# The last batch's second product by seven products of halves

## The chip, the cores and the metric

The kernel runs on one core of one Trainium2 chip. The metric is the device time of a whole run in microseconds; three runs of the kernel before gave 647.86, 649.02 and 649.75, so its time is the median, 649.02. The engines are PE (matrix products; PEld is its weight load), DVE (vector), ACT (scalar), POOL (GpSimd) and SP, whose queue issues every DMA of this kernel.

## The reference

Four batches of 768 positions and 512 channels go through an attention and then through a two-layer block. With float32 arrays throughout:

```
x  = attention(q, k, v)                 # banded, plus 24 block summaries; 8 heads of 64
h  = x.transpose(0,2,1) @ U @ V         # mixing over the positions, rank 32
u  = x + h.transpose(0,2,1)
ch = max(u @ w_ch1, 0) @ w_ch2          # 512 -> 2048 -> 512
return u + ch
```

The change is about `max(u @ w_ch1, 0) @ w_ch2`, the second product, for the last of the four batches. As a product of matrices it is 512 channels by 2048 hidden rows by 768 positions.

## The kernel before, in words

A float32 factor is used as two parts, a rounded high one and the rest (`hi`, `lo`), and each product is three matmuls: high by high, high by low, low by high. So every weight and every activation has to be split: ACT copies the high part into a rounding type, and another engine subtracts it for the low part.

Batch 0 runs both products directly while the weights are still arriving, and stores what the later batches need to DRAM: the first layer's weights with four sums of halves (`up_there`), and the second layer's weights (`down_there`). Batches 1 to 3 each run two phases.

- `up_phase` is the first product, already by seven products of halves instead of eight (Winograd's form of Strassen's scheme). The hidden rows go in eight pairs p; each pair takes seven products of six matmuls of 384 columns. A result is four blocks of 128x384 in `st.h[p]`. Two products of the last pair, `third` and `second`, are left over at its end and run among the first steps of the next phase.
- `down_phase` is the second product, direct. For each of 16 blocks f of 128 hidden rows, four output tiles of 512 columns and two of 2x256 (in the last batch four of 256) are accumulated in six to eight PSUM banks; the positions are 768 = 512 + 256. `gate_high` (line 1284, ACT) and `gate_low` (line 1288, DVE) make the two parts of max(h, 0) for the next f, in two buffers `gh` and `gl` of their own. `leave` (line 1339, DVE) adds u and sends the outputs.

The weights of both phases come back from DRAM as `whole` tiles of up to 512 KB by `fetch_weight` (line 884, three buffers) and are split into units of 128x512 by `prepare` (lines 179 and 180: the high part on ACT, the low part on POOL; eight buffers). `prepare` is called once for every unit that is used, so four units are ready ahead of use. `tick` fetches the next `whole` a few steps after the second unit of one is split.

The order on every engine is the order in which this code is written: nothing reorders it, and each engine works through its own queue, waiting on semaphores. While a batch runs its two phases, the attention of the next batch is spread between their steps (`later_steps`); the last batch has none beside it. The eight PSUM banks, and the buffers named `w…`, `op…` and `h…`, are used in turn by different tiles; a new user waits until the last reader of the old tile is done.

## Time and profile before

| | |
|---|---|
| three runs, median | 649.02 us (647.86 to 649.75) |
| the profiled execution | 648.17 us, of which the profile's span is 646.4 us |
| PE busy in the span | 627.1 us (97%), 5528 matmuls |
| DVE, ACT, POOL busy | 361.7, 354.6 and 363.3 us (55 to 56%) |
| the chain that ended last | PE 87%, DMA 4%, DVE 3% |
| granted TensorE clock | 1.00 in all stages |

The span is what lies between the first and the last instruction; 1.77 us of the run's own time lie around it. In a matmul row of the profile the duration is that from start to end of one matmul, and matmuls overlap, so what a matmul costs is read from a stretch with many of them: its length over their count. The stages of the span: batch 0 until about 216 us, batch 1 from there to 366, batch 2 to 517, batch 3 to the end; the last batch's first product is at 517 to 574 and its second at 574 to 643.

### The profile page before, as it was taken

How to read it: one execution, taken by the hardware profiler on the slowest of the kernel's cores; microseconds unless marked ns; L12 is line 12 of the kernel's file. 1: busy time of each engine (PE TensorE's matmuls, PEld its weight loads, DVE VectorE, ACT ScalarE, POOL GpSimd, SP SyncE). 2: the span in 40 equal slices, each digit the busy share in tenths (PEclk: the TensorE clock that was granted, in tenths of full speed). 3: DMA queues.
4: the chain of work that ended last, by engine and by line, in shares of the span. 5: the costliest groups of instructions: out<-in, count | busy, mean ns of one | idle time of the engine just before them, and what ended most of it. 6: DMA issues, size and time to landing. Idle time of an engine off the chain costs nothing.

```text
span 646.4 us, 14559 instructions
## 1 busy us (share of the span) xinstructions
PE 627.1 (97%) x5528; PEld 563.4 (87%) x5528; DVE 361.7 (56%) x1002; ACT 354.6 (55%) x788; POOL 363.3 (56%) x391
## 2 busy tenths in 40 slices
PE   5879999999999999999999999999999999999997
PEld 4669988888888899998888899998888899998886
DVE  5779767675857596566444645565544522242223
ACT  4756766656663657675453457775453455553321
POOL 3525977965766875862246765771344565653320
PEclk9999999999999999999999999999999999999999
DMA  9897588866675169896628367887431164342002
GB/s 236 223 380 222 160 296 267 229 201 189 214 232 176 46 213 290 243 265 174 180 78 218 113 204 222 258 258 203 144 116 58 60 183 142 115 131 66 32 1 99
DMA packets 68678, 115.39 MB, mean 179 GB/s; under 512 B 6912, under 2 KB 43648, under 8 KB 68608
## 3 DMA queue, kind: packets, MB, share of 16 engines
q1 hardware_dynamic: 68608, 114.45, 58.9%
q8 instruction: 44, 0.72, 0.5%
q14 instruction: 26, 0.21, 0.1%
HBM read 90.31 MB, written 24.12 MB: 177 GB/s over the span
## 4 chain that ended last, share of the span: by engine, by line
PE 87%; DMA 4%; DVE 3%; SPq 2%; ACT 2%; issue 1%; DVEq 0%; ACTq 0%
PE acc L1316 30%; PE ps_h L1215 27%; PE acc L949 10%; PE ps_h L927 9%; PE ps_x L490 3%; PE ps_s L374 2%; PE ps_s L351 2%; DMA place<-in_w 1%; PE ps_t L460 1%; SPq L215 1%; DMA kt<-in_k 1%; PE ps_u L699 1%; DMA place<-in_v 1%; DMA place<-in_q 1%; PE ps_m L665 1%
## 5 line engine op out<-in xcount | busy, mean ns | idle before, releaser
L180 POOL TENSOR_TENSOR parts<-whole,parts 128x512 fp32r<-128x512 f32 (+1 forms) x144 | 182.3, 1273 | 162.9 <-ACT parts L179 153.1
L1316 PE MATMUL acc<-gh,parts 128*128 128x256 f32 (+1 forms) x768 | 198.2, 340 | 0.0
L1215 PE MATMUL ps_h<-op,parts 128*128 128x384 f32 x1008 | 181.7, 337 | 0.1
L1215 PEld LDWEIGHTS ps_h<-op,parts 128*128 128x128 f32 x1008 | 174.3, 188 | 2.7 <-issue 1.1
L1316 PEld LDWEIGHTS acc<-gh,parts 128*128 128x128 f32 x768 | 132.9, 189 | 17.4 <-issue 1.7
L1316 PE MATMUL acc<-gl,parts 128*128 128x256 f32 (+1 forms) x384 | 129.8, 338 | 0.2
L1288 DVE SCALAR_TENSOR_TENSOR gl<-place,gh 128x768 fp32r<-128x768 f32 x48 | 55.3, 1151 | 71.3 <-ACT gh L1284 71.2
L179 ACT CAST parts<-whole 128x512 fp32r<-128x512 f32 (+1 forms) x144 | 83.3, 583 | 3.3 <-DMA whole<-up 1.0
L1316 PEld LDWEIGHTS acc<-gl,parts 128*128 128x128 f32 x384 | 72.8, 189 | 7.5 <-DVE gl L1288 0.8
L410 ACT ACTIVATE e<-e,neg 128x120 f32<-128x120 f32 x144 | 46.5, 386 | 51.4 <-DVE neg L400 46.9
L927 PE MATMUL ps_h<-place 128*128 128x384 f32 x384 | 74.3, 342 | 0.0
L1284 ACT ACTIVATE gh<-place 128x768 fp32r<-128x768 f32 x48 | 40.5, 844 | 57.1 <-PE acc L1316 48.5
L927 PEld LDWEIGHTS ps_h<-place 128*128 128x128 f32 x384 | 66.2, 188 | 1.4 <-issue 0.4
L949 PE MATMUL acc<-place,gh 128*128 128x512 f32 x192 | 67.3, 405 | 0.0
L155 POOL TENSOR_SCALAR val<-place 128x512 f32<-128x512 f32 (+1 forms) x30 | 47.7, 1607 | 25.9 <-ACT place L142 21.4
L180 POOL TENSOR_TENSOR place<-val,place 128x512 fp32r<-128x512 f32 x29 | 38.7, 1357 | 18.3 <-ACT place L179 18.3
L742 POOL TENSOR_TENSOR op<-tmp,op 128x384 fp32r<-128x384 f32 x24 | 26.3, 1108 | 32.9 <-ACT op L738 30.2
L949 PEld LDWEIGHTS acc<-place,gh 128*128 128x128 f32 x192 | 35.9, 188 | 7.6 <-POOL place L180 0.6
L400 DVE CUSTOM_DVE_ANT_0 e<-ps_s,mask_sb 128x120 f32<-128x120 f32 x144 | 32.8, 277 | 11.3 <-PE ps_s L351 5.9
L949 PE MATMUL acc<-place,gl 128*128 128x512 f32 x96 | 37.7, 393 | 0.1
L161 DVE SCALAR_TENSOR_TENSOR val<-place,val 128x512 int32<-128x512 int32 (+1 forms) x33 | 31.7, 965 | 3.3 <-POOL val L155 3.2
L1241 DVE TENSOR_TENSOR place<-place,ps_h 128x384 f32<-128x384 f32 x24 | 13.2, 551 | 36.2 <-PE ps_h L1215 36.2
(113 smaller groups left out, 796.5 us busy)
## 6 DMA issues: line engine op xcount, KB each, us to landing
place<-in_w SPq DMA_DIRECT2D x32, 512.0 KB, 5.6
whole<-up SPq DMA_DIRECT2D x24, 512.0 KB, 4.4
whole<-down SPq DMA_DIRECT2D x24, 512.0 KB, 4.3
whole<-up SPq DMA_DIRECT2D x24, 384.0 KB, 3.4
vt<-in_v SPq DMA_DIRECT2D x48, 146.2 KB, 3.8
kt<-in_k SPq DMA_DIRECT2D x24, 288.0 KB, 5.9
there<-squares SPq DMA_DIRECT2D x16, 384.0 KB, 4.3
at<-there SPq DMA_DIRECT2D x64, 96.0 KB, 3.5
```

What stands on the lines that cost most here:

```text
L155: nc.gpsimd.tensor_scalar(f32(bits), f32(hi), 0.0, None, ALU.mult)
L161: lambda lo, hi, bits: nc.vector.scalar_tensor_tensor(bits, lo, 29, bits, ALU.logical_shift_right, ALU.bitwise_or),
L179: nc.scalar.copy(hi, val)
L180: engine.tensor_tensor(lo, val, f32(hi), ALU.subtract)
L400: nc.vector.tensor_tensor_reduce(out=e[:, u, :], in0=ps[:, i * KC : (i + 1) * KC], in1=mask_sb[:, m, :], scale=-SCALE, scalar=BIG, op0=ALU ...
L410: nc.scalar.activation(e[:, u, :], e[:, u, :], AF.Exp, bias=st.neg[h][:, u : u + 1], scale=-1.0,)
L927: nc.tensor.matmul(ps[:, :NH], w_split[0, f][:, c % 2, part_w, c // 2], ut[:, c, :], start=(n == 0), stop=(n == 3 * NC - 1),)
L949: nc.tensor.matmul(acc[t], gt[:, sl], w_split[1, f][:, part_w], start=(first and j == 0), stop=(last and j == 2),)
L1215: nc.tensor.matmul(ps, a[:, sa, i], b[:, sb, i], start=(first and n == 0), stop=(n == 5), skip_group_check=not first,)
L1284: nc.scalar.activation(gh, h, AF.Relu)
L1288: nc.vector.scalar_tensor_tensor(gl, h, 0.0, f32(gh), ALU.max, ALU.subtract)
L1316: nc.tensor.matmul(place, w[:, part_w, c * P : (c + 1) * P], gt[:, q0:q1], start=(f == 0 and i == 0 and j == 0), stop=(f == NF - 1 and j = ...
```

## The change

The last batch's second product is done by the same seven-product form. The 16 hidden blocks are taken as eight pairs, the output channels and the positions as two halves each, so that a pair's weights are blocks B11, B12, B21, B22 of 128x256 and its activations four blocks of 128x384. The products run one after the other (`SEVEN`), each over all eight pairs: a step n = (product k, pair p) is six matmuls of 384 columns, and there are 56 steps. Sums are kept in six PSUM banks (x, y, z, two channel blocks each), and three of them carry on from one product to a later one.

- *Weights.* During batch 1's `down_phase`, `sum_down` makes T1 to T4 of every pair on POOL, four subtractions of 128x256, into `op` and `h` buffers that are free then, and SP stores them (line 960). During batch 2's `down_phase` the split parts of B11, B21 and B22 are stored as they are, three DMAs of 256 KB a pair. The last batch loads the B units ready split (one 512 KB DMA for a unit of two pairs, line 933) and the T sums whole; their high part is ACT's as before, their low part DVE's (line 949) and no longer POOL's, one step later.
- *Activations.* `gate_sums` (lines 1410 to 1415) takes the place of the gate for a pair: three max(h, 0) of 128x384 on ACT in place, and three sums on DVE. It runs in the last `up_phase`, one pair behind. In each step of the new phase the operand is split: high part on ACT (line 1433), low part on DVE (line 1440), up to twelve steps ahead, in 18 buffers. One more sum of each pair (`fourth_sum`, line 1444) is made in product 3.
- *Outputs.* Each half of a channel block is begun and ended by a DVE addition of 128x384 (lines 1465 and 1472) and sent as 192 KB.

PE's queue in the last phase, first as it was (a tile of 512 positions and one of 256; `acc` are the output tiles):

```order
L1316 MATMUL acc_7505<-gh,parts 128x512
L1316 MATMUL acc_7505<-gl,parts 128x512
L1316 MATMUL acc_7505<-gh,parts 128x512
L1316 MATMUL acc_7516<-gh,parts 128x256
L1316 MATMUL acc_7516<-gl,parts 128x256
L1316 MATMUL acc_7516<-gh,parts 128x256
```

These stand among 384 such matmuls, 192 of each width. As they are now, from the end of the last `up_phase` (L1291) on:

```order
L1291 MATMUL ps_h<-op,parts 128x384 x324
L1501 MATMUL acc<-gh,parts 128x384 x6
L1291 MATMUL ps_h<-op,parts 128x384 x6
L1501 MATMUL acc<-gl,parts 128x384 x6
L1291 MATMUL ps_h<-op,parts 128x384 x6
L1501 MATMUL acc<-gh,parts 128x384 x6
L1501 MATMUL acc<-gl,parts 128x384 x6
L1501 MATMUL acc<-gh,parts 128x384 x6
L1501 MATMUL acc<-place,parts 128x384 x60
```

The 192 matmuls of 512 columns and 192 of 256 have become 336 of 384, with the two left-over products between the first steps.

DVE's queue in the last phase held 14 subtractions of 768 columns in a row and eight output additions. Now, around the start of product 3 (L1440 is an operand's low part, L1444 a fourth sum, L949 a weight's low part, L1465 an output begun):

```order
L1440 TENSOR_TENSOR place_7641<-place_7362,place_7641 128x384
L1444 TENSOR_TENSOR place_7137<-place_7137,x_7004 128x384
L1440 TENSOR_TENSOR place_7641<-place_7437,place_7641 128x384
L1444 TENSOR_TENSOR place_7212<-place_7212,x_7004 128x384
L949 TENSOR_TENSOR parts_7913<-whole_7826,parts_7913 128x512
L1440 TENSOR_TENSOR gl_7552<-place_7512,gl_7552 128x384
L1444 TENSOR_TENSOR place_7287<-place_7287,qz0_84 128x384
L1440 TENSOR_TENSOR gh_7549<-place_7007,gh_7549 128x384
L1444 TENSOR_TENSOR place_7362<-place_7362,qz1_85 128x384
L949 TENSOR_TENSOR parts_7936<-whole_7866,parts_7936 128x512
```

Two steps, twelve matmuls, now bring DVE five operations here; before, one f with its 24 matmuls brought it one of 768 columns.

SP's queue at the same place, where there were eight loads of `down` and the outputs (B_107 to B_109 are the stored parts of B11, B21 and B22):

```order
L912 DMA whole<-sums 128x1024 [waits DMAHW5_49,Pool_49]
L912 DMA whole<-sums 128x1024 [waits DMAHW6_49,Pool_49]
L933 DMA parts<-B_107 128x2x512 [waits PE_49]
L912 DMA whole<-sums 128x1024 [waits DMAHW7_49,Pool_49]
L933 DMA parts<-B_107 128x2x512 [waits PE_49] x2
L933 DMA parts<-B_107 128x2x512
L933 DMA parts<-B_108 128x2x512
L933 DMA parts<-B_108 128x2x512 [waits DMAHW0_49,PE_49]
L933 DMA parts<-B_108 128x2x512 [waits DMAHW1_49,PE_49]
L933 DMA parts<-B_108 128x2x512 [waits DMAHW2_49]
L912 DMA whole<-sums 128x1024 [waits DMAHW3_49,DVE_49]
```

The B units stand right behind each other, each behind the wait for the buffer that it fills. The diff, cut to its core:

```diff
 BLOCKS = ("A11", "A12", "S2", "S1", "S3", "S4", "A22")
+SEVEN = (
+    ("A11", "B11"),
+    ("A12", "B21"),
+    ("S2", "T2"),
+    ("S1", "T1"),
+    ("S3", "T3"),
+    ("S4", "B22"),
+    ("A22", "T4"),
+)
+NH2 = DM // 2
...
+    for b in range(1, B):
...
+        if b < B - 1:
+            for p in range(NF // 2):
+                from_whole(down_there[p].rearrange("p t c -> p (t c)"), ("down", 2 * p), ("down", 2 * p + 1))
+            continue
+        for n, (_, name) in enumerate(SEVEN):
+            for p in range(0, NF // 2, 4):
+                keys = [("part", n, p), ("part", n, p + 2)]
+                if name[0] == "T":
+                    from_whole(sums_there[int(name[1]) - 1, :, p : p + 4], *keys)
+                else:
+                    units += [(key, None, name) for key in keys]
...
     def prepare():
 
+        finish_lows()
         n = len(prepared)
         if n == len(units):
             return
-        key = units[n]
-        second = key[0] in ("S0", "D") or key[0] == "down" and key[1] % 2 == 1
-        whole = fetched[n // 2][:, DM:] if second else fetched[n // 2][:, :DM]
+        key, load, second = units[n]
+        if load is None:
+            t = wt.tile([P, 2 * DM], F32R, name="parts", tag=unit_tags[n % 8])
+            t = t.rearrange("p (s c) -> p s c", s=2)
+            there = halves_there[second][:, :, key[2] : key[2] + 2]
+            nc.sync.dma_start(out=f32(t), in_=there.rearrange("p s a c -> p s (a c)"))
+            prepared.append((key, t))
+            return
...
-        split(hi, lo, whole, nc.gpsimd)
         prepared.append((key, t))
-        if second:
-            due.append(4)
+
+        def low():
+            engine = nc.vector if key[0] == "part" else nc.gpsimd
+            engine.tensor_tensor(lo, whole, f32(hi), ALU.subtract)
+            if second:
+                due.append(4)
+
+        nc.scalar.copy(hi, whole)
+        if key[0] == "part":
+            lows.append(low)
+        else:
+            low()
+        while unsent and unsent[0][0] <= n:
+            _, to, at = unsent.pop(0)
+            nc.sync.dma_start(out=to, in_=at)
+        if key[0] == "down":
+            p = key[1] // 2
+            if n < len(units) // 3 and second:
+                sums = sum_down(p, fetched[load])
+                unsent.append((n + 4, sums_there[:, :, p].rearrange("k p c -> p k c"), sums))
+            if n > len(units) // 3:
+                for r in range(2):
+                    name = f"B{1 + second}{1 + r}"
+                    if name in halves_there:
+                        unsent.append((n + 3, halves_there[name][:, :, p], f32(t)[:, :, r * NH2 : (r + 1) * NH2]))
+
+    def sum_down(p, whole):
+
+        t = op_place(p) if p < 4 else hidden_place(p - 4)
+        t = t[:, : 4 * NH2].rearrange("p (k c) -> p k c", c=NH2)
+        b11, b12, b21, b22 = (whole[:, j * NH2 : (j + 1) * NH2] for j in range(4))
+        t1, t2, t3, t4 = (t[:, k] for k in range(4))
+        nc.gpsimd.tensor_tensor(t1, b12, b11, ALU.subtract)
+        nc.gpsimd.tensor_tensor(t3, b12, b22, ALU.subtract)
+        nc.gpsimd.tensor_tensor(t2, b22, t1, ALU.subtract)
+        nc.gpsimd.tensor_tensor(t4, b21, t2, ALU.subtract)
+        return t
...
+    def gate_sums(st, p):
+
+        a11, a12, a21, a22 = (st.h[p][:, f, r * NH : (r + 1) * NH] for r in range(2) for f in range(2))
+        s1, s2 = (st.places.pop(0) for _ in range(2))
+        nc.scalar.activation(a11, a11, AF.Relu)
+        nc.scalar.activation(a22, a22, AF.Relu)
+        nc.scalar.activation(a12, a12, AF.Relu)
+        nc.vector.scalar_tensor_tensor(s1, a21, 0.0, a22, ALU.max, ALU.add)
+        nc.vector.scalar_tensor_tensor(a21, a21, 0.0, a11, ALU.max, ALU.subtract)
+        nc.vector.tensor_tensor(s2, s1, a11, ALU.subtract)
+        st.blocks[p] = {"A11": a11, "A12": a12, "S3": a21, "A22": a22, "S1": s1, "S2": s2, "S4": a12}
...
+    def part_high(st, n):
+
+        k, p = divmod(n, NF // 2)
+        t = st.slots.pop(0)
+        hi, lo = t[:, :NH], t[:, NH:]
+        nc.scalar.copy(hi, st.blocks[p][SEVEN[k][0]])
+        return hi, lo, t
+
+    def part_low(st, n, hi, lo):
+
+        k, p = divmod(n, NF // 2)
+        val = st.blocks[p][SEVEN[k][0]]
+        nc.vector.tensor_tensor(lo, val, f32(hi), ALU.subtract)
+
+    def fourth_sum(st, p):
+        a12 = st.blocks[p]["A12"]
+        nc.vector.tensor_tensor(a12, a12, st.blocks[p]["S2"], ALU.subtract)
...
+        def finished(k, i):
+            x, y, z = (sums.get((name, i)) for name in "xyz")
+            if k == 0:
+                begin((0, i), x, 0, i)
+            elif k == 1:
+                end((0, i), y, 0, i)
+            elif k == 2:
+                begin((1, i), x, 0, 2 + i)
+            elif k == 3:
+                begin((2, i), z, 1, 2 + i)
+            elif k == 4:
+                end((2, i), x, 1, 2 + i)
+            elif k == 5:
+                end((1, i), z, 0, 2 + i)
+            else:
+                begin((3, i), x, 1, i)
+                send((3, i), 1, i)
+
+        def part(n, i):
+            k, p = divmod(n, NF // 2)
+            name = "xyxzxzx"[k]
+            if (name, i) not in sums:
+                sums[name, i] = half_bank("acc")
+            ps, w, g = sums[name, i], ready[n][0], ready[n][1]
+            off = (p % 2) * NH2 + i * P
+            for j, (part_w, part_g) in enumerate(((0, 0), (0, 1), (1, 0))):
+                nc.tensor.matmul(
+                    ps,
+                    w[:, part_w, off : off + P],
+                    g[part_g],
+                    start=((name, i) not in begun and j == 0),
+                    stop=(p == NF // 2 - 1 and j == 2),
+                    skip_group_check=True,
+                )
+            begun.add((name, i))
...
+        def begin_gates(last):
+            for _ in range(2):
+                if len(gates) <= min(last, n_all - 1) and st.slots:
+                    n = len(gates)
+                    gates.append(part_high(st, n))
+                    behind.append(n)
...
+        for n in range(n_all):
+            k, p = divmod(n, NF // 2)
+            if p % 2 == 0:
+                w = use_weight("part", k, p)
+            finish_gates(min(len(behind), max(0, len(gates) - 1 - n)))
+            ready[n] = (w, gates[n])
+            if n < n_all - 2:
+                part(n, 0)
+                part(n, 1)
+                st.slots.append(gates[n][2])
+            elif n == n_all - 1:
+                for i in range(2):
+                    part(n - 1, i)
+                    part(n, i)
+            finish_gates(0)
+            if k == 3:
+                fourth_sum(st, p)
+            if n in (0, 2):
+                for j in ((0, 1, 3, 4, 5), (2, 6))[n // 2]:
+                    t = op_place(j).bitcast(F32R)
+                    st.slots += [t[:, i * S : (i + 1) * S] for i in range(2)]
+            begin_gates(min(n + GATES_AHEAD, NF // 2 - 2 if n < 4 else n_all))
+            if p % 2 == 0:
+                prepare()
+            else:
+                finish_lows()
+            yield
...
+        if not ahead:
+            sum_places(cur)
+            for p in range(NF // 2 - 1):
+                steps.setdefault(7 * p + 11, []).append((gate_sums, cur, p))
...
+            if i == UP - 4 and not ahead:
+                phase7 = seven_phase(cur)
+                next(phase7)
+        if not ahead:
+            for i, _ in enumerate(phase7):
+                if i < 2:
+                    do([last[i]])
+                if i == 3:
+                    gate_sums(cur, NF // 2 - 1)
+                tick()
+            break
```

More of the change, by code (lines that the diff above doesn't have):

```diff
@@ L834, in body @@
     up_there = [dram.tile([P, 14 * P], F32, name=f"up{p}", bufs=1) for p in range(NF // 2)]
-    down_there = [dram.tile([P, 2, DM], F32, name=f"down{p}", bufs=1) for p in range(NF // 2)]
+    down_there = dram.tile([NF // 2, P, 2, DM], F32, name="down", bufs=1)
+    halves_there = {
+        name: dram.tile([P, 2, NF // 2, NH2], F32, name=name, bufs=1) for name in ("B11", "B21", "B22")
+    }
+    sums_there = dram.tile([4, P, NF // 2, DM // 2], F32, name="sums", bufs=1)
     def sum_weights(p, n):
@@ L860, in store_down @@
     def store_down(f):
-        nc.sync.dma_start(out=down_there[f // 2][:, f % 2], in_=w_kept["down", f])
+        nc.sync.dma_start(out=down_there[f // 2, :, f % 2], in_=w_kept["down", f])
     def store_sums(p):
@@ L891, in prepare @@
             return
-        key = units[n]
-        second = key[0] in ("S0", "D") or key[0] == "down" and key[1] % 2 == 1
-        whole = fetched[n // 2][:, DM:] if second else fetched[n // 2][:, :DM]
+        key, load, second = units[n]
[6 more added lines that the diff above has]
+            return
+        whole = fetched[load][:, DM:] if second else fetched[load][:, :DM]
         t = wt.tile([P, 2 * DM], F32R, name="parts", tag=unit_tags[n % 8])[:, : 2 * whole.shape[-1]]
-        if key[0] == "down":
+        if key[0] in ("down", "part"):
             t = t.rearrange("p (s c) -> p s c", s=2)
@@ L918, in use_weight @@
         used.append(key)
-        return t if key[0] == "down" else [t[:, i] for i in range(t.shape[1])]
+        return t if key[0] in ("down", "part") else [t[:, i] for i in range(t.shape[1])]
     def up(st, hf, f):
@@ new lines, in sum_places @@
+    def sum_places(st):
+        ts = [mo.tile([P, NU, DM], F32, name="x").rearrange("p u c -> p (u c)")]
+        ts += [z.rearrange("p u q -> p (u q)") for z in qz]
+        for tag in ("squares", "at"):
+            t = att.tile([P, 4, NU, 32], F32, name=tag, tag=tag, bufs=1)
+            ts.append(t.rearrange("p i u q -> p (i u q)"))
+        st.places = [t[:, j * NH : (j + 1) * NH] for t in ts for j in range(t.shape[1] // NH)]
+        st.blocks = {}
+    def part_high(st, n):
[4 more added lines that the diff above has]
+        return hi, lo, t
```

66 lines of the change are left out of this document (50 added, 16 removed).

## The prediction

> **What bounds the kernel now.** First the page's busy times:
>
> ```profile
> PE 627.1 (97%) x5528; PEld 563.4 (87%) x5528; DVE 361.7 (56%) x1002; ACT 354.6 (55%) x788; POOL 363.3 (56%) x391
> ```
>
> PE is busy in all but 3% of the span and the others in little over half of it, so the question for the last batch is whether PE waits there for anything. The chain of waits in order of time, from the last batch on:
>
> ```profile
> 517.52 56.16 PE ps_h L1215 x324
> 573.68 1.39 PE acc L1316 x6
> 575.07 1.04 PE ps_h L1215 x6
> 576.12 1.39 PE acc L1316 x6
> 577.50 1.04 PE ps_h L1215 x6
> 578.55 64.12 PE acc L1316 x372
> 642.67 0.02 issue
> 642.69 0.42 DVE o L1339
> ```
>
> The chain never leaves PE: 129 us of matmuls without a gap, then one addition and the last store. The last batch ends when its matmuls have been issued. A matmul of 384 columns costs 56.16 / 324 = 0.1733 us with a weight load of its own each time; the second product costs 1.39 + 1.39 + 64.12 = 66.90 us for 384 matmuls of 512 and 256 columns.
>
> **The change, part by part.**
>
> *PE.* 66.90 us go. 336 matmuls of 384 columns come, of the shape that the last `up_phase` issues: 336 x 0.1733 = 58.23 us. The two left-over products stay. That is -8.67 us where PE is never kept waiting. What lies between is what each step needs in time; let T be the end of the last `up_phase` (573.68 in the profile before). A step is 1.04 us, and with `third` and `second` between the first ones step n (from 2 on) begins at T + 2.08 + 1.04 n.
>
> *DVE in the new phase* is the closest. From T until the weight part that step 38 uses, its queue holds 64 operations of 384 columns (operand parts, fourth sums, outputs, the last two pairs' sums) and 12 of 512. What one costs:
>
> ```profile
> 49.68 1.95 DVE L720 TENSOR_TENSOR place<-ps_u,place 128x384 fp32r<-128x384 f32 x4
> 51.55 1.28 DVE L164 SCALAR_TENSOR_TENSOR val<-place,val 128x512 int32<-128x512 int32 x2
> ...
> 54.15 1.28 DVE L180 TENSOR_TENSOR place<-val,place 128x512 fp32r<-128x512 f32 x2
> 55.35 0.55 DVE L940 SCALAR_TENSOR_TENSOR gl<-ps_h,gh 128x384 fp32r<-128x384 f32 x1
> ```
>
> Four of 384 columns start at 49.68 and the next kind at 51.55: 0.47 us apart. Two of 512 from 54.15, the next at 55.35: 0.60 apart. Their durations are longer than that:
>
> ```profile
> L1254 DVE TENSOR_TENSOR place<-place,ps_h x24: 514/554/555, 220.8 to 568.6; 128x384 f32<-128x384 f32 x24
> L180 DVE TENSOR_TENSOR place<-val,place x3: 676/680/693, 49.0 to 54.7; 128x512 fp32r<-128x512 f32 x3
> ```
>
> So one starts before the one ahead of it ends. By starts, 64 x 0.47 + 12 x 0.60 = 37.3 us, from about T + 1.4 (DVE waits for three max(h, 0) on ACT first), and about 1.5 us in which DVE waits for product 0 to end before it can begin the outputs: done at T + 40.2. Step 38 begins at T + 2.08 + 39.5 = T + 41.6. That is 1.4 us in time, and the earlier weight parts have 2 to 4 us. By durations, 64 x 0.554 + 12 x 0.680 = 43.6, plus 1.4: T + 45.0, with no idle time left, so 3.4 us late. I take the starts, since these rows are the same operations in a row. After step 38 the fourth sums are over and DVE gains on PE again.
>
> The Trainium skill, "VectorE: DVE Perf Modes", section "The DRAIN you can't avoid", says that the next DVE operation does not start until the pipe of the one ahead has emptied, whatever the semaphores; by that rule the sum is the one by durations. The rows above speak against it, with starts 0.08 us before the end; it is a rival below.
>
> *ACT.* Four rows of the last `up_phase`:
>
> ```profile
> 521.05 1.14 ACT L179 CAST parts<-whole 128x512 fp32r<-128x512 f32 x2
> ...
> 530.04 0.48 ACT L1274 COPY place<-ps_h 128x384 f32<-128x384 f32 x1 [1.41 <-PE ps_h L1215]
> 530.41 0.41 ACT L179 CAST parts<-whole 128x256 fp32r<-128x256 f32 x1
> 531.08 0.48 ACT L1249 COPY place<-ps_h 128x384 f32<-128x384 f32 x1 [0.26 <-PE ps_h L1215]
> ```
>
> Copies of 384 are 0.37 apart from what follows, casts of 512 take 0.62 and start 0.52 apart. The change puts three max(h, 0) of 384 columns (some 0.42 each) between the copy at 530.04 and that at 531.08. That second copy frees the bank for the fourth product of the pair, two products (2.08 us) after its own: it would be done at about 530.04 + 0.37 + 0.30 + 1.26 + 0.48 = 532.45, and PE wants it at 533.16 or so. Nothing is lost; with 0.7 us more on ACT it would be 1.04 us a pair at most. In the new phase ACT has 0.42 + 0.52/2 = 0.68 of 1.04 us a step. DVE's sums in `up_phase` (three more beside three of 0.55 in 7.28 us) are hidden.
>
> *Tail.* The last output addition is 0.55 and not 0.42 us, and its store larger:
>
> ```profile
> out_t<-o SPq DMA_DIRECT2D x8, 192.0 KB, 1.9
> out_t<-o SPq DMA_DIRECT2D x4, 128.0 KB, 1.8
> ```
>
> +0.13 + 0.1 = +0.23 us.
>
> *Batches 1 and 2.* They get work and lose none. In batch 1's second product POOL gets 32 subtractions of 128x256:
>
> ```profile
> L261 POOL TENSOR_TENSOR place<-place 128x256 f32<-128x256 f32 x12 | 11.2, 934 | 0.0
> ...
> 285.00:366.00 81.00, 80.89 (x776) 69.32 (x775) 42.25 (x105) 42.41 (x85) 36.42 (x35) 1.00 0.56 156
> ```
>
> 32 x 0.93 = 30 us on top of 36.4 of 81: it fits, and the units split by POOL are used four f later, some 17 us. But a DVE operation beside a POOL one takes longer:
>
> ```profile
> 306.57 1.94 DVE L1288 SCALAR_TENSOR_TENSOR gl<-place,gh 128x768 fp32r<-128x768 f32 x1
> 310.95 0.96 DVE L1288 SCALAR_TENSOR_TENSOR gl<-place,gh 128x768 fp32r<-128x768 f32 x1 [1.80 <-ACT gh L1284]
> ```
>
> 1 us more on the operand of the next f, in up to 16 f. PE gets it 1 us or more before use in most; where ACT is late too (the operands for the next batch) it would wait some tenths. I take +0.5 us, between 0 (nothing there can get faster) and 2. SP gets 8 stores of 512 KB in batch 1 and 24 of 256 KB in batch 2, ahead of attention loads; they start a load late only where SP has no idle time, and I count them in this 0.5.
>
> *Sum against the profiled execution:* 648.17 - 8.67 + 0.23 + 0.5 = 640.2 us, of which 1.77 lie around the span (646.4). The median of the runs is 0.85 above that execution: 641.1 us.
>
> **The rivals.**
>
> 1. *DVE takes durations.* Then PE waits from about step 33 to 38, 3.4 us in all: 644.5 us. For it: the operations depend on ACT parts by semaphores, and the margin by starts is only 1.4 us. Against it: the four rows above.
> 2. *The loads arrive late.* Near T four B units of 512 KB are let go within some 1.1 us, since SP stands before the buffer of the last pair but one. Step 4 wants the third unit at T + 6.2.
>
> ```profile
> GB/s 236 223 380 222 160 296 267 229 201 189 214 232 176 46 213 290 243 265 174 180 78 218 113 204 222 258 258 203 144 116 58 60 183 142 115 131 66 32 1 99
> ```
>
> At 290 GB/s 2.1 MB take 7.2 us from T - 2.1, so T + 5.1; at 176, one of the slower busy slices, 11.9, T + 9.8 and 3.6 us late: 644.7. Against it: other traffic is near nothing there (66 and 32 GB/s).
> 3. *Slower than before.* The place is the fetch of the turned attention weights (`at`) in batches 1 and 2, behind SP's new stores and beside them:
>
> ```profile
> 422.19 2.60 SPq L443 DMA_DIRECT2D at<-there  x4
> 446.20 1.91 SPq L443 DMA_DIRECT2D at<-there  x4
> 455.14 1.83 SPq L443 DMA_DIRECT2D at<-there  x4
> DMA to landing us min/median/max: 2.1/2.9/6.7
> 429.35 0.82 PE ps_x L490 x48
> 451.83 0.82 PE ps_x L490 x48
> 462.61 0.82 PE ps_x L490 x48
> ```
>
> Landing at 2.9 us, PE's use follows 1.7, 0.8 and 2.7 us later. Were each to land at the worst, 6.7, PE would wait 2.1 + 3.0 + 1.1 = 6.2 us in each of two batches: 641.1 + 12.4 = 653.5 us. It decides from landings of about 6 us on: 1.4 + 2.3 + 0.4 = 4.1 a batch is the 8 us won. Against it: in batch 2's stretch the slices move 60 to 203 GB/s, far from full.
> 4. *The matmuls don't get fewer in time*, that is, a step of six costs more than 1.04 us because each needs a freshly split operand: at 1.19 us a step (66.9 / 56) nothing is won, 649.6 with tail and disturbance. Against it: `up_phase` alternates operands and weights in the same way at 0.1733.
>
> **How the numbers follow.** Forecast 0.70; DVE by durations 0.12; late loads 0.07; slower by `at` 0.06; no gain 0.05. The predicted time is the forecast's, 641.1 us. Its own range is 639.3 (641.1 less the disturbance of 0.5 and 1.2, by which the lowest run before lay below the median, rounded down) to 643; for the first two rivals and the bound of 2 us on the disturbance the range goes up to 645.4. With this kernel a difference under 0.3%, 1.95 us, can't be told from none: faster is below 647.1, slower above 651.0. The forecast and the first two rivals are all faster (0.89, of which I move 0.02 to the middle for several losses at once): faster 0.87, same 0.07, slower 0.06.
>
> **What would show it.** Right: in the chain of waits some 56 steps of L1501 follow each other on PE in 58 to 59 us, without DVE, ACT or DMA between them; L1440 starts 0.47 us after the one before; batch 1's end, at 366 before, is less than 1 us later, and batch 2's (517) no more. Wrong: DVE L949 or L1440 ahead of PE's L1501 around steps 32 to 38 (rival 1), DMA `parts` ahead of the first steps (rival 2), DMA `at` ahead of ps_x in batches 1 and 2 (rival 3), L1501 alone at more than 0.18 us a matmul (rival 4). An idle PE at another place than these would make the prediction wrong in its working, whatever the time.

## The result

Six runs of the changed kernel gave a median of 639.01 us (638.06 to 642.04); six of the kernel before 649.21. The ratio is 0.9852, with a 95% interval of 0.9828 to 0.9877: faster, by some 9.6 us (the medians differ by 10.2). A second comparison on another occasion (in the experiments) gave 0.9888, 0.9863 to 0.9913. The forecast was 641.1.

The profiled execution took 638.37 us, its span 636.6. Its busy times, and the chain of waits in order of time from the last batch on (start and length in us, engine, tile, line, count; `issue` is time in which the engine waited for nothing that the profile shows):

```profile
PE 618.2 (97%) x5480; PEld 562.8 (88%) x5480; DVE 401.3 (63%) x1096; ACT 374.3 (59%) x852; POOL 364.2 (57%) x407
```

```profile
516.54 56.16 PE ps_h L1291 x324
572.70 1.04 PE acc L1501 x6
573.74 1.04 PE ps_h L1291 x6
574.78 1.04 PE acc L1501 x6
575.82 1.04 PE ps_h L1291 x6
576.86 56.18 PE acc L1501 x324
633.04 0.02 issue
633.06 0.56 DVE o L1465
```

The last batch is still PE without a gap. Its first product takes 56.16 us as before. The second takes 1.04 + 1.04 + 56.18 = 58.26 us instead of 66.90, and 56.18 / 324 is 0.1734 us a matmul, as in the rows before.

To see where the rest of the 9.80 us between the two profiled executions lies, cut both chains at the same places: the start of batch 1, of its second product, of batch 2, of batch 3, and PE's end. For the changed kernel the first three are the starts of these rows of its chain, and batch 3 starts at 516.54, above:

```profile
216.34 3.15 PE ps_h L1291 x18
...
284.23 0.70 PE acc L1389 x3
...
368.63 5.21 PE ps_h L1291 x30
```

The table has the differences, in us, for these two and for all kernels run later. "Last batch" goes to the end of PE's last matmul.

| kernel | batch 0 | batch 1, first product | batch 1, second product | batch 2 | last batch |
|---|---|---|---|---|---|
| before | 218.58 | 66.97 | 84.09 | 147.88 | 125.15 |
| changed | 216.34 | 67.89 | 84.40 | 147.91 | 116.50 |
| changed, once more | 219.30 | 66.91 | 84.45 | 147.89 | 116.50 |
| side work alone | 219.10 | 66.91 | 84.59 | 147.87 | 125.15 |
| last phase alone | 215.43 | 66.92 | 84.10 | 147.89 | 116.50 |
| 8 DVE repetitions | 220.63 | 66.93 | 84.59 | 147.90 | 119.46 |
| 16 DVE repetitions | 218.84 | 66.94 | 84.67 | 148.26 | 124.20 |
| 16, set apart | 219.97 | 66.97 | 84.46 | 147.90 | 122.22 |
| low parts on POOL | 216.12 | 66.94 | 84.79 | 147.90 | 122.28 |
| stores twice | 217.06 | 66.96 | 85.13 | 148.09 | 116.50 |
| B loads twice | 218.87 | 66.92 | 84.73 | 147.87 | 161.80 |
| B traffic | 215.94 | 66.95 | 84.86 | 147.89 | 127.30 |
| weight loads later | 218.30 | 66.92 | 84.48 | 147.89 | 116.50 |
| both later | 215.93 | 66.93 | 84.09 | 147.90 | 116.50 |

Read this by columns. Before and changed differ by -2.24 + 0.92 + 0.31 + 0.03 - 8.65, and -0.17 after PE's end: -9.80. The last batch's 8.65 us are the change. Batch 0's -2.24 are not: all kernels have the same instructions there, and the column runs from 215.43 to 220.63. The spread lies in the first 52 to 58 us, up to the first matmul of batch 0's second product, where PE waits for the input loads; from that matmul on to batch 1 all fourteen profiles take 162.65 to 163.03 us. In five of the fourteen (neither before nor changed) the granted clock is also 0.5 for 3.4 us in that first part. So where the input loads fall moves a run by more than anything else here. The 0.92 is of the same kind: one late load of a weight in batch 1's first product, which no other run shows.

### The profile page after: what moved, and what is told of

Same layout as the page of the kernel before. It is cut to its first block, busy times and chain, and to the rows that moved or that the text cites. A ratio compares the mean times of both kernels' runs of the same rounds, so it can differ in the third digit from the quotient of the medians.

```text
span 636.6 us, 14752 instructions
## 1 busy us (share of the span) xinstructions
PE 618.2 (97%) x5480; PEld 562.8 (88%) x5480; DVE 401.3 (63%) x1096; ACT 374.3 (59%) x852; POOL 364.2 (57%) x407
## 4 chain that ended last, share of the span: by engine, by line
PE 87%; DMA 4%; DVE 4%; SPq 2%; ACT 2%; issue 1%; POOL 0%; DVEq 0%; ACTq 0%
PE ps_h L1291 26%; PE acc L1389 21%; PE acc L1025 10%; PE acc L1501 9%; PE ps_h L1003 9%; PE ps_x L500 3%; PE ps_s L384 2%; PE ps_s L361 2%; PE ps_t L470 2%; DMA place<-in_k 1%; DMA whole<-up 1%; PE ps_u L709 1%; DMA place<-in_v 1%; SPq L225 1%; PE ps_m L675 1%
## 5 line engine op out<-in xcount | busy, mean ns | idle before, releaser
L949 POOL TENSOR_TENSOR parts<-whole,parts 128x512 fp32r<-128x512 f32 (+1 forms) x128 | 159.1, 1250 | 111.2 <-ACT parts L953 107.5
L1291 PE MATMUL ps_h<-op,parts 128*128 128x384 f32 x1008 | 182.0, 337 | 0.7 <-ACT place L1337 0.6
L1291 PEld LDWEIGHTS ps_h<-op,parts 128*128 128x128 f32 x1008 | 174.3, 188 | 3.5 <-issue 1.1
L1389 PE MATMUL acc<-gh,parts 128*128 128x256 f32 (+1 forms) x512 | 135.1, 342 | 0.0
L1389 PEld LDWEIGHTS acc<-gh,parts 128*128 128x128 f32 x512 | 88.9, 189 | 12.2 <-issue 1.7
L1389 PE MATMUL acc<-gl,parts 128*128 128x512 f32 (+1 forms) x256 | 86.6, 338 | 0.1
L1364 DVE SCALAR_TENSOR_TENSOR gl<-place,gh 128x768 fp32r<-128x768 f32 x32 | 38.5, 1202 | 25.9 <-ACT gh L1360 25.8
L1389 PEld LDWEIGHTS acc<-gl,parts 128*128 128x128 f32 x256 | 48.5, 189 | 5.0 <-DVE gl L1364 0.8
L1501 PE MATMUL acc<-place,parts 128*128 128x384 f32 x246 | 43.6, 334 | 0.0
L1501 PEld LDWEIGHTS acc<-place,parts 128*128 128x128 f32 x246 | 42.7, 188 | 0.0
L1025 PE MATMUL acc<-place,gl 128*128 128x512 f32 x96 | 37.7, 393 | 0.1
L1360 ACT ACTIVATE gh<-place 128x768 fp32r<-128x768 f32 x32 | 27.0, 843 | 16.4 <-PE acc L1389 10.8
```

What stands on the lines that cost most here:

```text
L949: engine.tensor_tensor(lo, whole, f32(hi), ALU.subtract)
L1025: nc.tensor.matmul(acc[t], gt[:, sl], w_split[1, f][:, part_w], start=(first and j == 0), stop=(last and j == 2),)
L1291: nc.tensor.matmul(ps, a[:, sa, i], b[:, sb, i], start=(first and n == 0), stop=(n == 5), skip_group_check=not first,)
L1364: nc.vector.scalar_tensor_tensor(gl, h, 0.0, f32(gh), ALU.max, ALU.subtract)
L1389: nc.tensor.matmul(place, w[:, part_w, c * P : (c + 1) * P], gt[:, q0:q1], start=(f == 0 and i == 0 and j == 0), stop=(f == NF - 1 and j = ...
L1501: nc.tensor.matmul(ps, w[:, part_w, off : off + P], g[part_g], start=((name, i) not in begun and j == 0), stop=(p == NF // 2 - 1 and j == ...
```

## The experiments

### The pieces apart

Theory A took the stages for the whole account: 8.65 us in the last phase, 0.3 lost in batch 1. Theory B took the medians at their word: another 1.7 us won by something in the earlier stages. Three kernels ran side by side with the kernel before: the changed one, the side work without its use, and the use without the side work.

The changed kernel:

> The changed kernel once more, beside the two kernels that follow. Theory A: the whole gain is the last phase, 69.0 us before and 60.3 after in the two traces (-8.65), the tail adds 0.14, and batch 1's second product is 0.3 us longer; what the medians showed beyond that (-10.2 in all) is where the input loads of batch 0 fell. Then this run is 8.5 us faster than the kernel before (8 to 9), about 640.7 if that is 649.2. Theory B: the side work or the new program also makes an earlier stage faster by some 1.7 us: 10.2 us faster, about 639.0.

The side work alone is the kernel before with this added to its weight preparation:

```diff
+        if key[0] == "down":
+            p = key[1] // 2
+            if n < len(units) // 3 and second:
+                sums = sum_down(p, fetched[n // 2])
+                unsent.append((n + 4, sums_there[:, :, p].rearrange("k p c -> p k c"), sums))
...
```

> The side work alone: in batch 1 the four sums of every pair on POOL and their stores, in batch 2 the stores of the split parts, nobody reads them, and the last batch's second product is the direct one of the kernel before. Theory A: 0.3 us slower than before (0 to 1), since the second product of batch 1 took 84.40 instead of 84.09 us in the traces, and batch 2's 0.03 longer. Theory B (an earlier stage gets faster by the side work): 1.7 us faster. My price ahead of the result was +0.5, with 2 as its upper end.

The last phase alone is the changed kernel without those lines, with its loads turned to what batch 0 has stored:

```diff
-                    from_whole(sums_there[int(name[1]) - 1, :, p : p + 4], *keys)
+                    from_whole(down_there[2 * int(name[1]) - 2 + p // 4].rearrange("p t c -> p (t c)"), *keys)
...
-            nc.sync.dma_start(out=f32(t), in_=there.rearrange("p s a c -> p s (a c)"))
+            nc.sync.dma_start(out=f32(t), in_=down_there[(key[1] + key[2] // 2) % 8])
```

> The last phase alone: the sums and split parts are neither made nor stored in batches 1 and 2; the last batch loads tiles of the same size from the stored second layer's weights in their place, so its outputs are not the reference's. Theory A: 8.5 us faster than before plus what the side work cost: 8.8 us faster (8.3 to 9.3), 0.3 faster than the changed kernel beside it. Theory B: 1.7 us slower than the changed kernel beside it.

Against the kernel before (median 646.77): the changed one 640.07, ratio 0.9888 (0.9863 to 0.9913); the side work 648.62, 1.0018 (0.9998 to 1.0039); the last phase alone 637.62, 0.9868 (0.9838 to 0.9897). The side work makes nothing faster, and the last phase alone is not slower than the whole: theory B falls. The stages agree with A: 84.59 in one place and 125.15 in another for the side work, 84.10 and 116.50 for the last phase alone. The size of A's 0.3 was low. The second product of batch 1 is 0.31 to 0.77 us longer, 0.53 on average, in the profiles of the nine kernels that have the side work as the change has it ("stores twice" and the two "later" ones left out).

### How much room DVE has

In the changed kernel the weight part of step 38 is the place that the prediction called closest. The timeline of DVE there (start, length, line, tiles, shape; "x2" are two in a row):

```profile
607.97 0.55 DVE L1444 TENSOR_TENSOR place<-place,qz 128x384 f32<-128x384 f32 x1
608.43 0.69 DVE L949 TENSOR_TENSOR parts<-whole,parts 128x512 fp32r<-128x512 f32 x1
609.04 0.55 DVE L1440 TENSOR_TENSOR place<-place 128x384 fp32r<-128x384 f32 x1
609.51 0.55 DVE L1444 TENSOR_TENSOR place<-place,squares 128x384 f32<-128x384 f32 x1
609.98 1.02 DVE L1465 TENSOR_TENSOR o<-acc,x 128x384 f32<-128x384 f32 x2
610.91 0.55 DVE L1440 TENSOR_TENSOR place<-place 128x384 fp32r<-128x384 f32 x1
611.37 0.56 DVE L1444 TENSOR_TENSOR place<-place,at 128x384 f32<-128x384 f32 x1
611.84 0.69 DVE L949 TENSOR_TENSOR parts<-whole,parts 128x512 fp32r<-128x512 f32 x1
```

DVE takes one operation after the other without idle time, 0.47 us from start to start for 384 columns and 0.60 for 512. The last row is the twelfth weight part, done at 612.53; step 38 begins at 576.86 + 36 x 1.04 = 614.30. So 1.8 us are left. Is it the queue that decides? Then more operations ahead of that row must cost PE what exceeds 1.8 us.

```diff
         nc.vector.tensor_tensor(lo, val, f32(hi), ALU.subtract)
+        if 24 <= n < 32:
+            nc.vector.tensor_tensor(lo, val, f32(hi), ALU.subtract)
```

> The subtraction of the operand's low part is done twice for the eight operands of product 3 (steps 24 to 31): eight more DVE operations of 384 columns ahead of the weight part of step 38 in its queue. In the changed kernel's trace that weight part is done at 612.53 us, 1.8 us before step 38 begins (572.70 + 41.6 = 614.3). Theory: DVE takes an operation every 0.47 us and is never idle there, so 8 x 0.47 = 3.8 us come, 1.8 are cover, and PE waits 2.0 us in product 4: 2.0 us slower than the changed kernel. Rival 'durations': 8 x 0.554 = 4.4, 2.6 slower. Rival 'there is other slack' (the queue does not decide): no change.

With `n < 40` in place of 32:

> The same for the sixteen operands of products 3 and 4 (steps 24 to 39). Theory: 16 x 0.47 = 7.5 us less 1.8 of cover: 5.7 us slower than the changed kernel, the wait falling in products 3 and 4. By durations 16 x 0.554 - 1.8 = 7.1 slower. Other slack: no change.

The last batch took 119.46 and 124.20 us, 2.96 and 7.70 longer, and PE waited for DVE's weight parts (the chain leaves DVE, at a `parts` of L949, for the last 106 of the 336 matmuls: at the third matmul of step 38, the first that uses the weight's low part). So the queue decides and nothing else covers it. But neither number fits: 2.0 and 5.7 were expected by starts, and the durations give 2.6 and 7.1. DVE's timeline with the sixteen repetitions (L1442) shows why:

```profile
600.59 0.69 DVE L949 TENSOR_TENSOR parts<-whole,parts 128x512 fp32r<-128x512 f32 x1
601.19 0.55 DVE L1440 TENSOR_TENSOR place<-qz,place 128x384 fp32r<-128x384 f32 x1
601.78 0.56 DVE L1442 TENSOR_TENSOR place<-qz,place 128x384 fp32r<-128x384 f32 x1
602.25 0.55 DVE L1440 TENSOR_TENSOR place<-squares,place 128x384 fp32r<-128x384 f32 x1
602.84 0.56 DVE L1442 TENSOR_TENSOR place<-squares,place 128x384 fp32r<-128x384 f32 x1
```

A repetition writes what the operation ahead of it has just written, has to wait for DVE's own semaphore, and starts 0.59 us after it: when it has ended. The next operation, which depends on neither, starts 0.47 later. So a repetition costs 0.59: 8 x 0.59 - 1.8 = 2.9 and 16 x 0.59 - 1.8 = 7.6, close to 2.96 and 7.70. (In the trace of the changed kernel that third matmul starts at 614.49, 1.96 us after the weight part is done; a wait costs PE 0.05 us ahead of it and 0.12 behind it, which leaves 1.8.) That was a reading made after the fact, so it was put to a test of its own: the same sixteen, each repeating the operand one before.

```diff
+        if 24 <= n < 40:
+            k, p = divmod(n - 1, NF // 2)
+            hi, lo = st.parts_of[n - 1]
+            nc.vector.tensor_tensor(lo, st.blocks[p][SEVEN[k][0]], f32(hi), ALU.subtract)
```

> As the run with sixteen repeated low parts, but each repetition is that of the operand before, so that it does not write what the operation right ahead of it has just written. With the repetition right behind, the last phase (end of batch 2 to the end on PE) grew by 7.70 us over the changed kernel's 116.50, and each repetition began 0.58 and not 0.47 us after its predecessor. Theory (an operation that depends on the one ahead waits for its end, one that does not starts 0.08 earlier): 16 x 0.47 - 1.8 = 5.7 longer, 122.2. Rival (a longer queue costs 0.59 an operation whatever it writes): 7.7 longer, 124.2.

The last batch took 122.22 us. In the timeline the repetitions (L1445) now keep the pace of the others:

```profile
601.16 0.55 DVE L1441 TENSOR_TENSOR place<-qz,place 128x384 fp32r<-128x384 f32 x1
601.63 0.55 DVE L1445 TENSOR_TENSOR place<-qz,place 128x384 fp32r<-128x384 f32 x1
602.10 0.55 DVE L1441 TENSOR_TENSOR place<-squares,place 128x384 fp32r<-128x384 f32 x1
602.57 0.55 DVE L1445 TENSOR_TENSOR place<-qz,place 128x384 fp32r<-128x384 f32 x1
```

So DVE's queue is counted by starts for operations that do not depend on the one right ahead, and by durations and 0.04 us more for those that do. In time against the kernel before: 8 repetitions 0.992 (0.9897 to 0.9943), 16 of them 0.9998 (0.9973 to 1.0022): sixteen operations in the wrong place would have eaten the gain.

### The low parts on POOL

POOL has nothing to do in the last phase. The edit:

```diff
-            engine = nc.vector if key[0] == "part" else nc.gpsimd
+            engine = nc.gpsimd
```

> The low parts of the T weights on POOL, which has nothing to do in the last phase, instead of DVE. Theory: DVE is off the path by 1.8 us already, so time does not change (within 0.3 us of the changed kernel), and DVE's weight-free queue reaches the end of product 4's operands some us earlier. Rival 'contention': a 768-column DVE operation took 0.96 us alone and 1.94 beside POOL in the kernel before; 12 POOL operations of 1.25 us up to step 38 would cost DVE 7.5 us of its 30 while it is spared 12 x 0.60 = 7.2, so the gain in DVE's queue would be about nothing, and a weight part waits for a slower POOL: 0 to 1 us slower.

It took 644.49 us, ratio 0.9953 (0.9932 to 0.9974), and the last batch 122.28 us, 5.78 longer. Both expectations were too low. The chain of waits of this run, from the middle of the phase:

```profile
576.08 28.26 PE acc L1501 x162
604.34 0.02 POOLq L949
604.36 0.02 issue
604.38 7.13 POOL parts L949
611.51 0.04 issue
611.55 26.47 PE acc L1501 x142
```

One subtraction of 128x512 took 7.13 us on POOL; the quickest took 1.30. PE stood still for 3.75 us of it, from 607.80 to 611.55. But the wait is not the whole 5.78. From 613.1 on the granted clock was 0.50 for 3.4 us (the view by stretches: bounds and length; busy time and count of PE, PEld, DVE, ACT, POOL; clock; share of the DMA engines; GB/s):

```profile
613.10:616.50 3.40, 3.40 (x12) 3.40 (x11) 3.40 (x3) 2.80 (x7) 3.07 (x2) 0.50 0.60 177
```

The matmuls start 0.32 us apart there instead of 0.1734, which makes 1.6 us; the wait, from start to start, makes 4.0. Why the clock fell is not shown; in the DVE runs and under "B traffic" below, waits of PE of up to 1.5 and 2.2 us left it at 1.00 in the phase. DVE's timeline at the same time, and further ahead, where POOL had come first:

```profile
586.35 1.65 DVE L1440 TENSOR_TENSOR gh<-x,gh 128x384 fp32r<-128x384 f32 x1
587.92 4.80 DVE L1440 TENSOR_TENSOR place<-x,place 128x384 fp32r<-128x384 f32 x3
...
604.67 0.55 DVE L1440 TENSOR_TENSOR place<-place 128x384 fp32r<-128x384 f32 x1
...
609.82 0.55 DVE L1444 TENSOR_TENSOR place<-place,squares 128x384 f32<-128x384 f32 x1
610.29 1.01 DVE L1465 TENSOR_TENSOR o<-acc,x 128x384 f32<-128x384 f32 x2
611.22 0.69 DVE L1440 TENSOR_TENSOR place<-place 128x384 fp32r<-128x384 f32 x1
611.84 1.64 DVE L1444 TENSOR_TENSOR place<-place,at 128x384 f32<-128x384 f32 x1
```

The two slow each other: at 586 a DVE operation takes 1.65 us instead of 0.55 while POOL is at work, and from 604.38 on DVE starts fourteen operations at full pace while POOL's one does not end. The rival had the contention, but let only DVE pay for it. The Trainium skill, "SBUF — State Buffer", section "Who interferes with whom", has a rule for such pairs: a DVE operation with two SBUF inputs contends with a GpSimd instruction that reads SBUF for ports that the two share, the lock is exclusive, and the order of issue decides which of them is held. DVE's 1.65 us agree with it. POOL's 7.13 go further than one operation's wait: twelve DVE operations with both inputs in SBUF went ahead, 0.47 us apart. The last two of the fourteen (L1465, from 610.29) read one input from PSUM, `acc`, and POOL's subtraction ended 1.2 us after the first of them began, about the 1.30 that it takes undisturbed; the DVE operation behind them, at 611.22, took 0.69 instead of 0.55. So it seems to have got in when two such operations came, and not at the end of one operation; one place in one trace shows it.

### The side work's 0.5 us

In batch 1's second product of the changed kernel PE waits once where the kernel before does not (start, length, what; in brackets the idle time ahead; a wait of 0.11 us ahead of an `acc` matmul 80 us on is in both):

```profile
293.11 0.89 PE L500 MATMUL ps_x<-vt,at 120*32 120x65 f32 x48 [0.21 <-issue]
```

That is a product with the turned attention weights `at`, the place of the prediction's third rival. The waits of SP's queue in this stretch (line waited, for whom; us in total, times, the longest):

```profile
SPq L915 <- POOL place L981: 18.5, 5, 6.0
SPq L445 <- DVE squares L440: 11.0, 3, 5.2
```

L915 is the load of the next second-layer weights. Its buffer is the one that POOL's sums (L978 to L981) still read, so SP stands before it, and the store and loads of the attention (L445, L453) stand behind:

```profile
286.00 0.33 SPq L915 DMA_DIRECT2D whole<-down  x1
286.42 0.38 SPq L445 DMA_DIRECT2D there<-squares  x1
286.89 2.52 SPq L453 DMA_DIRECT2D at<-there  x4
```

In the kernel before the loads of `at` were issued 0.27 us after this phase began (285.82 against 285.55), here 2.66 (286.89 against 284.23). First, is more traffic from the stores enough to make it worse?

```diff
                 unsent.append((n + 4, sums_there[:, :, p].rearrange("k p c -> p k c"), sums))
+                unsent.append((n + 4, sums_again[:, :, p].rearrange("k p c -> p k c"), sums))
...
                         unsent.append((n + 3, halves_there[name][:, :, p], at))
+                        unsent.append((n + 3, halves_again[name][:, :, p], at))
```

> Each store of the sums (batch 1) and of the split parts (batch 2) is issued twice, the second to another place: 8 x 512 KB and 24 x 256 KB more. It doubles what my rival 3 spoke of, SP's stores ahead of the attention loads. In the changed kernel's trace the loads of the turned attention weights took 3.5 us (median) and up to 7.4 us to land in batches 1 and 2, and PE waited 0.2 us for one. Theory: there is cover left, 0.3 us slower (0 to 1). Rival: the loads decide soon after, 4 us or more slower.

639.87 us, ratio 0.9897 (0.9858 to 0.9936). Batch 1's second product took 85.13 us, 0.5 over the mean of the nine (84.62) and 0.27 over the longest, and batch 2 0.2 more: within what was expected. PE waits twice there:

```profile
292.95 0.89 PE L500 MATMUL ps_x<-vt,at 120*32 120x65 f32 x48 [0.26 <-issue]
303.32 0.89 PE L500 MATMUL ps_x<-vt,at 120*32 120x65 f32 x48 [0.65 <-DMA at<-there]
```

Next, the weight load let go later, so that SP does not meet the busy buffer:

```diff
-                due.append(4)
+                due.append(8 if key[0] == "down" and n < len(units) // 3 else 4)
```

> In batch 1's second product the next weight load is let go eight steps after its buffer's last split instead of four, so that SP does not stand in front of a buffer that POOL still reads for the sums (in the changed kernel SP waited 18.5 us there in five waits), with the attention's store and loads behind it. Theory: the wait of PE for the turned attention weights (0.2 to 0.4 us, at the second ps_x of the phase) goes, and batch 1's second product takes 84.1 us as before the change instead of 84.40 to 84.45. In the run's time 0.3 us faster than the changed kernel, less than rounds can tell. Rival (the wait has another cause, the longer queue on POOL itself): 84.4 stays.

638.72 us, ratio 0.9865 (0.984 to 0.989), but the stage took 84.48 us: the expected 84.1 did not come. The wait at the second `ps_x` was gone and one at the third had come:

```profile
303.89 0.89 PE L500 MATMUL ps_x<-vt,at 120*32 120x65 f32 x48 [0.33 <-DMA at<-there]
```

The attention's store had gone out at 297.65, and at 295.50 a store of the sums, 512 KB, ahead of it. So the next kernel lets every sums store go one f later as well:

```diff
-                unsent.append((n + 4, sums_there[:, :, p].rearrange("k p c -> p k c"), sums))
+                unsent.append((n + 5, sums_there[:, :, p].rearrange("k p c -> p k c"), sums))
```

> The later weight loads of the run before this one (it removed PE's wait at the second ps_x of batch 1's second product, and put one of 0.33 us at the third, where a sums store of 512 KB had been issued 2 us ahead of the attention's store and its loads), and beside it every sums store one f later, so that it stands behind that attention load. Theory (what is left of the side work's cost is the landing of the turned attention weights): no wait of PE in batch 1, its second product 84.1 us instead of 84.40 to 84.48, the rest as in the changed kernel; in time 0.3 us faster than it, less than rounds tell. Rival (the cost is POOL's longer queue): 84.4 stays.

Batch 1's second product took 84.09 us, the number of the kernel before to the hundredth, with no wait of PE left but the 0.11 that the kernel before has too, and POOL's work as long as in the change (66.0 us in this stretch, 65.9 there, 40.5 before). The other profiles agree: in all nine with the side work PE waits at the second `ps_x`, in some also at the third, 0.2 to 0.65 us together, and what the stage is longer than 84.09 exceeds these waits by 0.15 at most; the kernel before and the last phase alone have no such wait. So the side work's cost is the landing of `at`, which the order on SP sets. The run's time, 640.09 us, ratio 0.9881 (0.985 to 0.9912), cannot show half a microsecond next to batch 0's spread; by the stages this is the fastest of the kernels that do the whole work (batch 1 to PE's end 415.42 us, the changed kernel's two profiles 416.70 and 415.75; the last phase alone, without the side work, 415.41).

### The loads at the start of the last phase

PE waits for no load there. How near is rival 2? In the changed kernel's trace each of the first eight B units lands 2.2 to 5.0 us before its first matmul; the third, of which the rival spoke, at T + 3.3, 2.8 us before step 4 uses it. More traffic was to show what happens without that margin.

```diff
             nc.sync.dma_start(out=f32(t), in_=there.rearrange("p s a c -> p s (a c)"))
+            nc.sync.dma_start(out=f32(t), in_=there.rearrange("p s a c -> p s (a c)"))
```

> Every load of a split B unit (512 KB) is issued twice into the same buffer, so that 7 MB instead of 3.7 are to come around the start of the last phase. My rival 2 spoke of loads that land late there. In the changed kernel PE waits for none of them; they land 5.2 to 9.9 us after issue. Theory: at the 290 GB/s that the fastest slices show, 7.3 MB and 1 MB of sums from 565 us on are in at 593, the eighth unit is used at T + 16.7 = 589.4: PE waits some 4 us (0 to 8) for DMA in the first sixteen steps. Rival (the loads are covered with a wide margin): no wait, the last phase stays at 116.5 us.

The last batch took 161.80 us, but not for the reason that the run was made for: the second load writes the buffer of the first, so SP waited for each first load to land (57.6 us in twelve waits); with PE waiting in between, the granted clock was 0.5 in some 37 us of that batch as well. It tells what a chain of unhidden landings costs, and nothing about traffic. The copy that nobody waits for does that:

```diff
             nc.sync.dma_start(out=f32(t), in_=there.rearrange("p s a c -> p s (a c)"))
+            beside = dram.tile([P, 2, DM], F32, name=f"beside{n}", bufs=1)
+            nc.sync.dma_start(out=beside, in_=there.rearrange("p s a c -> p s (a c)"))
```

> The loads of the split B units as in the changed kernel, and beside each a copy of the same 512 KB from DRAM to another place in DRAM that nobody waits for: 12 more transfers of 512 KB. The doubled load into the same buffer made SP wait for every first load's landing (57.6 us in twelve waits), so it showed what unhidden landings cost and not what traffic does. Theory: the B units' margin is some us; seven copies beside seven loads ahead of T + 17 are 3.7 MB more, at 290 GB/s 13 us of transfer in a stretch that moves about 190 GB/s of what it can: PE waits 0 to 8 us, 4 at the middle, at the first sixteen steps. Rival (wide margin): the last phase stays at 116.5 us.

The last batch took 127.30 us, 10.8 longer; at most 8 had been expected. The view by stretches, first the 18 us from 572 on in this run, then two stretches of the changed kernel, the 13 us in which its loads come and the 17.3 us from T on:

```profile
572.00:590.00 18.00, 13.37 (x71) 11.86 (x70) 13.95 (x29) 15.80 (x37) 0.00 (x0) 1.00 0.97 315
```

```profile
567.00:580.00 13.00, 13.00 (x77) 13.00 (x77) 9.94 (x21) 10.32 (x26) 0.06 (x1) 1.00 1.00 329
572.70:590.00 17.30, 17.30 (x101) 17.30 (x101) 15.63 (x32) 17.26 (x41) 0.00 (x0) 1.00 0.55 177
```

With the copies the DMA engines are full throughout (0.97), the B units land 11.1 us after issue (median) instead of 6.5, and from the second to the eighth each lands only 0.04 to 0.14 us before its first matmul: PE waits for them. In the changed kernel the engines are full too while the loads come (1.00 at 329 GB/s; the expectation's 290 was too low), and the 0.55 is a mean of that and of the idle engines from 584 on. So rival 2's mechanism is real. What keeps it off is not free bandwidth: it is that the loads start early enough, so that each unit is in 2.2 us or more before its use.

## Why the prediction was right, point by point

- **PE, -8.67 us.** The mechanism and the size were right. Measured -8.65: 116.50 instead of 125.15 us, in all six profiles in which the last phase was left as the change has it. Rival 4 (a dearer step) is out: 0.1734 us a matmul. (The "129 us of matmuls" beside the prediction's chain are 125.15 by its own rows; no term uses them.)
- **DVE by starts.** Forecast: the weight part of step 38 done at T + 40.2, step 38 at T + 41.6. Measured: 612.53 - 572.70 = T + 39.8, and T + 41.6. The sum came near by two misses that go against each other. The 64 and 12 operations begin at T + 1.4 as counted, but take 37.7 us and not 37.3, and the wait for product 0's end, taken as 1.5, is 0.77 in the trace:

```profile
582.69 1.08 DVE L1465 TENSOR_TENSOR o<-acc,x 128x384 f32<-128x384 f32 x2 [0.77 <-PE acc L1501]
```

- **Rival 1, DVE by durations.** False for this queue, where neighbours rarely depend on each other, and true for an operation that writes what the one ahead of it wrote (0.59 from start to start, against a duration of 0.55). The rule of the Trainium skill, "VectorE: DVE Perf Modes", section "The DRAIN you can't avoid", that the next operation starts only when the pipe is empty, does not hold here for the first kind: 0.47 us between starts with 0.55 each; the same section adds that a next operation that is not held starts earlier, which the prediction had left out and these rows agree with.
- **ACT and the last `up_phase`, nothing.** Right: 56.16 us as before.
- **The tail, +0.23.** Here a term of the sum was off. DVE's last addition is longer as forecast (0.56 after 0.42), but from PE's end to the span's end it is 3.73 us before and 3.56 in the changed kernel. The side work alone, which ends as the kernel before does, has 3.44, and the other profiles with the changed ending have 3.32 to 3.57: the two ends cannot be told apart.
- **Batches 1 and 2, +0.5.** The size was right (0.53 on average in batch 1's second product, and in batch 2 0.03 or less in eight of those nine profiles; the ninth, with sixteen repetitions, has 0.38, again with a wait of PE at a `ps_x`). The mechanism was not, so the size was luck. The prediction laid it on DVE's operand for the next f beside POOL; such an operation does take 1.67 us (at 286.37), and PE does not wait for it. What PE waits for is `at`, the third rival's place. That is one of the prediction's own signs of being wrong, in small. The prediction counted the new stores on SP, but not that an old entry of SP's queue, the weight load, now waits longer because POOL reads its buffer longer. With the two moves on SP, of that load and of the sums stores, the cost is gone.
- **Rival 2, late loads.** Did not happen: the loads are in 2.2 us or more before use, with the DMA engines full.
- **Rival 3, slower by `at`.** Right in the place; the size that it feared was not reached. It needed every `at` to land about 6 us after issue; in the changed kernel, from 290 us to batch 3, the longest took 7.4 and the median 3.5, and PE waits 0.2. With the stores doubled the stage grows by another 0.5.
- **The time.** 639.01 lies 2.1 us under the forecast and 0.3 under the low end of the range; taken by the ratio, 0.9852 x 649.02 = 639.4, it is just inside. The terms of the stages sum to about -8.65 + 0.53 and a tail that does not count, -8.1, where the prediction had -7.94. The first comparison came out at -9.6 and the second at -7.2, with intervals of -8.0 to -11.2 and -5.6 to -8.9; the sum lies in both. What is left fits the spread of batch 0, 5.2 us over the profiles with no difference in the instructions; that it is the whole rest in the runs, of which only one was profiled, is not shown. So how near a median comes to the forecast within some 2 us is luck; the stages are the test.

## What to carry to other kernels

Where PE never waits, a change that takes matmuls away is worth their count times their cost, and the work of the prediction is to find the queue with the least room and to count what stands ahead of one entry in it, by the distance of starts where neighbours are independent. When an engine reads a buffer longer than before, look for the load that waits to refill that buffer and for what stands behind this load in its queue: that place, and that of the added stores in the same queue, made the price of the side work. A mean share of the DMA engines says little about a burst: look at the stretch in which the loads come, and at how long before its use each one lands. When one stage of a run varies by more than the effect, compare the other stages between the profiles rather than the runs.

## What the runs showed of the hardware that was not expected

- DVE: an addition or subtraction of 128x384 that writes what the operation right ahead has written starts 0.59 us after it, 0.04 behind its end; with one operation between them it starts 0.47 after its neighbour, 0.08 ahead of its end.
- POOL beside a DVE that never idles: one subtraction of 128x512 took 7.13 us instead of 1.30, during which DVE went through twelve operations with both inputs in SBUF at its usual 0.47; it ended 1.2 us after DVE had begun two that read one input from PSUM.
- DMA: the 512 KB loads alone kept the engines at 1.00 and 329 GB/s for 13 us and landed after 6.5 us (median); beside DRAM to DRAM copies the engines moved 315 GB/s at 0.97 for 18 us, and the loads landed after 11.1.
- Clock: after a wait of PE of 3.75 us (low parts on POOL) the granted clock was 0.50 for 3.4 us and matmuls of 384 columns started 0.32 us apart instead of 0.1734; after waits of up to 2.2 us (B traffic) it stayed at 1.00.
